# Last layers: the first six pieces of w_out issued ahead of the second unit's tokens, with the pieces' tiles laid out in reverse

## The chip, the cores and the metric

One core of one Trainium2 chip runs the whole program. The metric is the device time of one execution in microseconds; lower is better.

## The reference, cut to what matters

```python
def reference(**kwargs):
    attn_out = _attn_ref(**attn_kwargs)                    # pooled-key attention, 4 x 8 heads x 576 rows
    x = np.ascontiguousarray(attn_out.transpose(0, 2, 1, 3)).reshape(B * S, H * D)   # 2304 x 512
    x = _moe_ref(x=x, **moe_kwargs)                        # top-1 of 8 experts, with a capacity
    return _moe2_ref(x=x, **moe2_kwargs)

def _moe2_ref(x, w_in, w_out, s, b):                       # the last layers
    h = x @ w_in                                           # 512 -> 2048
    r = np.maximum(h, 0.0)
    g = s * (r * r) + b
    return (g @ w_out).astype(np.float32)                  # 2048 -> 512
```

## The kernel before, in words

The program has three stages: attention with the routing, the expert layers (`Experts.main`), and the last layers (`last_layers`). The last layers work on units of 256 tokens (`CU`). The weight `w_out` comes in as 64-bit floats, in 16 pieces of 128 rows (512 KB each): every piece is loaded as pairs of 32-bit words into a tile `wo[i]`, turned into a 32-bit float by four steps on VectorE and one on ScalarE (`Weights64.step`, L735 to L744), and split by ScalarE (L1258) and GpSimd (L1259) into a high and a low part, which lie in the same memory under the same name.

Order is written out by hand (`manual_schedule`): each engine runs its instructions in the order of the program, and a DMA asked for with `nc.sync` is issued by SP, in order as well.

The seam between the stages goes so. `last` (L1166) is the end of the expert stage; it runs inside nested conditionals on the number of small units. It loads the first unit's tokens (`load_y(0)`, two DMAs: L899 reads 512 KB from `yt` into `yr`, L900 reads the row numbers `it` from `idc`), computes the last small unit's second layer (L1114), stores its result (`store_small`: L991 to `yt`, L992 from the tile `ids_s` to `idc`), then asks for the second unit's tokens (`load_y(1)`), and runs the first four first-layer tiles of unit 0 (`EARLY`, L912). After the conditionals join, `last_layers` issues two small loads for the scalars s and b (`sb`, L1441), and `rest(0)` runs `unit(2)`, which calls `pair()`. That first asks for all 16 pieces of `w_out` (L1320), then runs `first(0, ...)`: for each of 16 tiles f it does the first layer (L912), `square` (L1273 on ScalarE, L1274 on VectorE), one or two conversion steps of `w_out` (`spare`), and `parts` (L1279 ScalarE, L1280 GpSimd). After it `split_y(1, ...)` splits the second unit's tokens (L904, L905), and `second(0, ...)` multiplies by the converted pieces (L1285). When all 16 pieces are converted, `spare` goes on to sum them (L1306, L1308); that sum, with b, makes the rows of dropped tokens (L1313, L1314).

Memory: the expert stage's tiles lie in two pools, `m1` and `m`, which are given back when that stage ends. The pool `n` of the last layers (`sb`, `y1h`, `y1l`, `c_f`, `c_u`, `gh`, `gl`, `wo`) takes their place, in the order in which its tiles are declared. By the sizes of the tiles, all `wo` lie in what was `m`: before, `wo0` to `wo4` over `hs`, `xg`, `idt` and `ids_s`, `wo5` to `wo8` over `vraw` (the experts' second weight), `wo9` to `wo12` over `kraw` (the first weight) and `wo13` to `wo15` over `c_raw`.

Of the kernel before, what the change touches and what calls it, by code (L numbers as in the profile page):

```python
# [10 lines left out]
I32 = mybir.dt.int32  # L11
# [9 lines left out]
DM = H * D  # L21
# [3 lines left out]
P = 128  # L25
# [10 lines left out]
KF2 = FF2 // P  # L36
# [712 lines left out]
class Experts:  # L749
# [176 lines left out]
    def main(self, left, one, ps):  # L926


        nc, tc, yt = self.nc, self.tc, self.yt
# [69 lines left out]
        def conv(n, end=cv.total):  # L999
            for _ in range(n):  # L1000
                if pos[0] < end:
                    if pos[0] == 3 or pos[0] % 4 == 2 and pos[0] > 6:
                        self.load_raw(max(3, pos[0] // 4 + 2), queue)
                    cv.step(pos[0])
                    pos[0] += 1

        def part(n):
            for _ in range(n):
                if parted[0] < KF:
                    self.split_in(parted[0])  # L1010
                    parted[0] += 1
# [100 lines left out]
        def small_layer2(f):  # L1112
            for d in range(KD):
                nc.tensor.matmul(py[d][:, :SM], lhsT=self.w2r[:, f, d * P:d * P + P], rhs=hs[f], start=f == 0, stop=f == KF - 1)  # L1114

        def store_small(s):
            store_y(sid(s), yo(s % 2, SM), self.ids_s[s % 4], SM, SSUB)
# [48 lines left out]
        def last(s):  # L1166

            early = cap >= SM + CU
            if early:
                self.load_y(0)  # L1170
            for f in range(KF):
                small_layer2(f)
                if early and f in (4, 5):
                    for k in range(2):
                        self.split_y(0, 2 * f - 8 + k, nc.vector)
                conv(2)
                part(1)
            store_small(s)
            if early:
                self.load_y(1)  # L1180
            conv(cv.total)
            if not early:
                self.load_y(0)
                for k in range(KD):
                    self.split_y(0, k, nc.vector)
                self.load_y(1)
            for f in range(EARLY):
                self.layer1_y(0, ps[f], self.w1h[:, f], self.w1l[:, f])

# [43 lines left out]
def last_layers(nc, tc, c, a, pool, x, ps, out):  # L1233
# [6 lines left out]
    sb = pool.tile([P, 2], F32, name="sb")  # L1240
# [3 lines left out]
    cf, cu = [pool.tile([P, DM], I32, name=f"c_f{i}") for i in range(2)], [pool.tile([P, DM], F32, name="c_u0")]  # L1244
    gh = pool.tile([P, KF2, CU], F32R, name="gh")
    gl = pool.tile([P, KF2, CU], F32R, name="gl")
    wo = [pool.tile([P, DM, 2], I32, name=f"wo{i}") for i in range(KF2)]
    ph, po = ps[0:4], ps[4:8]
    sums = {}
    slots = raw[2:4]  # L1250
# [13 lines left out]
    def conv(n):  # L1264
        for _ in range(n):
            if done[0] < cv.total:
                cv.step(done[0])
                done[0] += 1

    def square(f, p, n):  # L1270

        r = rt[f % 4][:, :n]
        nc.scalar.activation(r, p, AF.Relu)  # L1273
        nc.vector.scalar_tensor_tensor(out=r, in0=p, scalar=0.0, in1=r, op0=ALU.max, op1=ALU.mult)  # L1274

    def parts(f, n=CU, at=None):

        at = f if at is None else at
        nc.scalar.copy(gh[:, at, :n], rt[f % 4][:, :n])  # L1279
        nc.gpsimd.tensor_sub(gl[:, at, :n], rt[f % 4][:, :n], gh[:, at, :n])  # L1280

    def layer2(p, j, f, c=slice(0, DM), at=None):
        at = f if at is None else at
        for i, (l, z) in enumerate(((gh, 0), (gh, 1), (gl, 0))):
            nc.tensor.matmul(p[:, c], lhsT=l[:, at, j * P:j * P + P], rhs=wo[f][:, z, c], start=f == 0 and i == 0, stop=f == KF2 - 1 and i == 2)  # L1285
# [12 lines left out]
    def tokens(u):  # L1298
        if u < NV:
            for k in range(KD):  # L1300
                x.split_y(u, k, nc.gpsimd)

    def add(i):

        if i == 0:
            nc.vector.tensor_add(sums["acc"], wo[0][:, 0], wo[0][:, 1])  # L1306
        elif 1 < i < 2 * KF2:
            nc.vector.tensor_add(sums["acc"], sums["acc"], wo[i // 2][:, i % 2])  # L1308
# [8 lines left out]
    def pair():  # L1317

        for i in range(KF2):
            nc.sync.dma_start(out=wo[i].rearrange("p c two -> p (c two)"), in_=wout[:, i])  # L1320
        held = []
        adds = iter(range(2 * KF2))

        def spare(n):
            for _ in range(n):
                if done[0] < cv.total:
                    conv(1)
                    continue
                if "acc" not in sums:
                    nc.vector.memset(onesf, 1.0)  # L1330
                    sums["acc"] = pool.tile([P, DM], F32, name="c_f0")
                    slots.append(pool.tile([P, DM], F32, name="c_f1"))
                    sums["drop"] = pool.tile([P, DM], F32, name="c_u0")
                add(next(adds, 2 * KF2))

        def first(u, f0, f1, banks):
            for n, f in enumerate(range(f0, f1)):
                p = banks[f % len(banks)][:, :CU]
                if u or f >= EARLY:
                    x.layer1_y(u, p, *win[f])  # L1340
                square(f, p, CU)
                spare(2 if u == 0 and n % 4 == 3 else 1)
                if held:
                    parts(*held.pop())
                held.append((f, CU, f))
            parts(*held.pop())

        def second(u, f0, f1, n):
            for f in range(f0, f1):
                for j in range(2):  # L1350
                    layer2(po[2 * u + j], j, f, at=f)
                spare(n)

        first(0, 0, KF2, ps)
        for k in range(KD):
            x.split_y(1, k, nc.gpsimd)
        second(0, 0, KF, 2)
        first(1, 0, KF, ph)
        x.load_y(2)
        second(1, 0, KF, 2)  # L1360
        second(0, KF, KF2, 2)
        first(1, KF, KF2, ph)
        tokens(2)
        second(1, KF, KF2, 2)
        for i in adds:
            add(i)
# [56 lines left out]
    def rest(u):  # L1423
        if u == NV:
            return
        if u < 2:
            rest(2)
            return
        if u < SURE:
            unit(u)  # L1430
            rest(u + 1)
            return
        with tc.If(kept > u * CU + P) as cond:
            unit(u)
            rest(u + 1)
        with cond.Else():
            with tc.If(kept > u * CU):
                half(u)

    for i, n in enumerate(("moe2_s", "moe2_b")):  # L1440
        nc.sync.dma_start(out=sb[:, i:i + 1], in_=a[n].unsqueeze(0).to_broadcast([P, 1]))  # L1441
    rest(0)


# [44 lines left out]
```

## Time and profile before

| | us |
|---|---|
| median of 3 runs | 723.9 (717.18, 723.9, 726.66) |
| the profiled execution | 719.65 |
| its span, first to last instruction | 718.0 |

| engine | busy us | share of the span |
|---|---|---|
| PE (TensorE matmul) | 603.5 | 84% |
| PEld (weight load) | 559.9 | 78% |
| DVE (VectorE) | 391.8 | 55% |
| POOL (GpSimd) | 324.3 | 45% |
| ACT (ScalarE) | 254.3 | 35% |

Times in a trace count from the start of the span. PEld overlaps PE. A DMA's row in the timeline is the time SP needs to issue it, not the transfer. PEclk is the granted TensorE clock as a share of full speed. "Issue" is time in which an engine waited for nothing that the profile shows. Releasers are inferred from semaphores: where an instruction waits for several, the one that came last is named.

### The profile page before, as it was taken

To read this page: it belongs to the slowest core of one execution; us is meant where nothing else is said; L and a number is where in the kernel's file an instruction comes from. 1 tells how busy PE (TensorE), PEld (TensorE's weight loads), DVE (VectorE), ACT (ScalarE), POOL (GpSimd) and SP (SyncE) were. 2 spreads that over 40 slices of the span, in tenths; PEclk is the share of its full clock that TensorE was granted. 3 is DMA by queue.
4 is the path that set the end of the run, shared out by engine and by line. 5 is a ranking of instruction groups with operands and counts; after the bars stand their busy time and mean duration, and the time that the engine had idled before them with its cause. 6 is when DMAs were issued, how large, how long until landed. Compare 5 with 4: busy or idle time off the path is not lost. (4 is left out here: it accounts for less than half of the span.)

```text
span 718.0 us, 11212 instructions
## 1 busy us (share of the span) xinstructions
PE 603.5 (84%) x3943; PEld 559.9 (78%) x3943; DVE 391.8 (55%) x793; ACT 254.3 (35%) x617; POOL 324.3 (45%) x336
## 2 busy tenths in 40 slices
PE   6788787768599387996976768989999999999985
PEld 5677776768499387996976647877989989899885
DVE  4789699749688482444520877999332212021250
ACT  1354655335254344414320544432412304123030
POOL 5567455465363343502300784644473515335281
PEclk8899989689889698997799778999999999999998
DMA  8997997792539766583812920001730010100000
GB/s 168 197 180 134 154 183 235 103 272 63 94 92 181 240 154 214 56 290 107 279 34 53 405 89 0 1 1 30 264 104 15 14 46 1 45 16 2 32 1 18
DMA packets 78571, 81.97 MB, mean 114 GB/s; under 512 B 30732, under 2 KB 59404, under 8 KB 78476
## 3 DMA queue, kind: packets, MB, share of 16 engines
q1 hardware_dynamic: 67580, 67.19, 37.1%
q0 software_dynamic: 3184, 6.83, 4.0%
q10 hardware_dynamic: 7712, 6.84, 3.2%
q8 instruction: 41, 0.67, 0.5%
q14 instruction: 54, 0.44, 0.3%
HBM read 64.04 MB, written 17.62 MB: 114 GB/s over the span
## 5 line engine op out<-in xcount | busy, mean ns | idle before, releaser
L1285 PE MATMUL bank<-wo,gh 128*128 128x512 f32 (+1 forms) x448 | 135.0, 384 | 13.7 <-POOL wo L1259 9.0
L1280 POOL TENSOR_TENSOR gl<-rt,gh 128x256 fp32r<-128x256 f32 (+1 forms) x112 | 89.3, 806 | 95.5 <-ACT gh L1279 88.9
L1285 PEld LDWEIGHTS bank<-wo,gh 128*128 128x128 f32 x448 | 83.4, 193 | 32.4 <-POOL wo L1259 11.1
L1285 PE MATMUL bank<-wo,gl 128*128 128x512 f32 (+1 forms) x224 | 85.3, 381 | 0.0
L791 POOL TENSOR_TENSOR w1l<-kraw,w1h 128x512 fp32r<-128x512 f32 x40 | 54.3, 1375 | 59.9 <-ACT w1h L790 59.6
L986 PE MATMUL bank<-hs,w2h 128*128 128x288 f32 (+1 forms) x308 | 72.9, 327 | 7.3 <-issue 7.3
L986 PEld LDWEIGHTS bank<-hs,w2h 128*128 128x128 f32 x308 | 55.2, 209 | 8.1 <-issue 7.8
L1292 DVE SCALAR_TENSOR_TENSOR raw<-bank,sb,c_u 128x512 f32<-128x512 f32 (+1 forms) x14 | 9.9, 710 | 85.4 <-PE bank L1285 85.4
L1273 ACT ACTIVATE rt<-tq 128x256 f32<-128x256 f32 (+1 forms) x26 | 9.5, 367 | 114.6 <-PE tq L912 92.1
L1285 PEld LDWEIGHTS bank<-wo,gl 128*128 128x128 f32 x224 | 43.2, 193 | 7.6
L986 PE MATMUL bank<-hs,w2l 128*128 128x288 f32 (+1 forms) x148 | 47.1, 318 | 2.1 <-DVE w2l L795 2.1
L1279 ACT CAST gh<-rt 128x256 fp32r<-128x256 f32 (+1 forms) x112 | 43.0, 384 | 4.1 <-DVE rt L1274 4.1
L1274 DVE SCALAR_TENSOR_TENSOR rt<-bank,rt 128x256 f32<-128x256 f32 (+1 forms) x60 | 24.1, 403 | 36.3 <-ACT rt L1273 36.3
L1293 POOL DMA_INDIRECT out_dram<-raw,it x12 | 12.0, 1000 | 62.3 <-DVE raw L1292 61.8
L1273 ACT ACTIVATE rt<-bank 128x256 f32<-128x256 f32 (+1 forms) x60 | 22.2, 370 | 39.5 <-PE bank L912 26.8
L1259 POOL TENSOR_TENSOR wo<-c_f,wo 128x512 fp32r<-128x512 f32 x16 | 24.8, 1550 | 21.5 <-ACT wo L1258 21.5
L798 POOL DMA_INDIRECT xg<-xd,idt x15 | 18.1, 1205 | 34.9 <-DMA idt<-ids 32.1
L986 PEld LDWEIGHTS bank<-hs,w2l 128*128 128x128 f32 x148 | 30.7, 207 | 2.4 <-DVE w2l L795 2.4
L795 DVE TENSOR_TENSOR w2l<-vraw,w2h 128x512 fp32r<-128x512 f32 x39 | 32.1, 823 | 0.5 <-ACT w2h L794 0.2
L210 PE MATMUL sc<-kbd,qT 128*128 128x144 f32 (+1 forms) x152 | 26.0, 322 | 2.3 <-DVE r L267 2.3
L744 DVE SCALAR_TENSOR_TENSOR c_f<-c_u,c_f 128x512 f32<-128x512 f32 x24 | 25.3, 1055 | 4.8 <-ACT c_u L737 3.5
L1308 DVE TENSOR_TENSOR c_f<-c_f,wo 128x512 f32<-128x512 f32 x30 | 26.2, 875 | 0.8
(409 smaller groups left out, 1706.7 us busy)
## 6 DMA issues: line engine op xcount, KB each, us to landing
kraw<-in_moe_w_dram SPq DMA_DIRECT2D x24, 512.0 KB
vraw<-in_moe_w_dram SPq DMA_DIRECT2D x24, 512.0 KB
wo<-in_moe_w_out_dram SPq DMA_DIRECT2D x16, 512.0 KB
c_raw<-in_moe_w_in_dram ACTq DMA_DIRECT2D x13, 512.0 KB
kraw<-in_k_dram SPq DMA_DIRECT2D x8, 576.0 KB
out_dram<-c_u SPq DMA_DIRECT2D x1, 4608.0 KB
q<-in_q_dram SPq DMA_DIRECT2D x16, 256.0 KB
xd<-xr SPq DMA_DIRECT2D x16, 256.0 KB
```

The costliest lines, as they stand in the source:

```text
L210: nc.tensor.matmul(sc[:n, p // 2, p % 2 * 144:p % 2 * 144 + 144], lhsT=q[:, p, :n], rhs=kbd[b % 2][:, p], start=True, stop=True)
L744: v.scalar_tensor_tensor(out=f, in0=u, scalar=TINY, in1=f, op0=ALU.is_ge, op1=ALU.mult)
L791: eng.tensor_sub(self.w1l[:, i], self.w1(i), self.w1h[:, i])
L795: eng.tensor_sub(self.w2l[i], self.w2r[:, i], self.w2h[i])
L986: nc.tensor.matmul(py[d][:, :v.n], lhsT=l[f][:, d * P:d * P + P], rhs=r[f], start=f == 0 and i == 0, stop=f == KF - 1 and i == 2)
L1259: nc.gpsimd.tensor_sub(w[:, 1], f, w[:, 0])
L1273: nc.scalar.activation(r, p, AF.Relu)
L1274: nc.vector.scalar_tensor_tensor(out=r, in0=p, scalar=0.0, in1=r, op0=ALU.max, op1=ALU.mult)
L1279: nc.scalar.copy(gh[:, at, :n], rt[f % 4][:, :n])
L1280: nc.gpsimd.tensor_sub(gl[:, at, :n], rt[f % 4][:, :n], gh[:, at, :n])
L1285: nc.tensor.matmul(p[:, c], lhsT=l[:, at, j * P:j * P + P], rhs=wo[f][:, z, c], start=f == 0 and i == 0, stop=f == KF2 - 1 and i == 2)
L1308: nc.vector.tensor_add(sums["acc"], sums["acc"], wo[i // 2][:, i % 2])
```

## The change

`load_y(1)` is taken out of `last` and issued in `pair()`, behind the sixth of the 16 loads of `w_out`. The two loads of `sb` move from the end of `last_layers` to just behind it. Loads 6 to 15 follow. The tiles `wo` are declared from 15 down to 0, so `wo0` to `wo2` lie where `c_raw` was, `wo3` to `wo6` over `kraw`, `wo7` to `wo10` over `vraw`, and `wo11` to `wo15` over the rest. No arithmetic changes.

```diff
@@ in last()
             store_small(s)
-            if early:
-                self.load_y(1)
             conv(cv.total)
             if not early:
                 self.load_y(0)
                 for k in range(KD):
                     self.split_y(0, k, nc.vector)
-                self.load_y(1)
@@ in last_layers()
-    wo = [pool.tile([P, DM, 2], I32, name=f"wo{i}") for i in range(KF2)]
+    wo = [pool.tile([P, DM, 2], I32, name=f"wo{i}") for i in reversed(range(KF2))][::-1]
@@ in pair()
         for i in range(KF2):
             nc.sync.dma_start(out=wo[i].rearrange("p c two -> p (c two)"), in_=wout[:, i])
+            if i == 5:
+                x.load_y(1)
+                for j, n in enumerate(("moe2_s", "moe2_b")):
+                    nc.sync.dma_start(out=sb[:, j:j + 1], in_=a[n].unsqueeze(0).to_broadcast([P, 1]))
@@ at the end of last_layers()
-    for i, n in enumerate(("moe2_s", "moe2_b")):
-        nc.sync.dma_start(out=sb[:, i:i + 1], in_=a[n].unsqueeze(0).to_broadcast([P, 1]))
     rest(0)
```

## Rows read from the trace of the kernel before

**Rows 1.** Chain of waits, 376 to 405 us: start us, length us, what
```profile
377.85 8.82 DMA idc<-ids_s
386.69 3.35 DMA it<-idc
...
390.43 0.03 SPq L1441
...
390.56 0.35 SPq L1441
...
391.43 5.45 DMA wo<-in_moe_w_out_dram
...
397.29 0.43 DVE c_f L735
```

**Rows 2.** Waits by engine, 376 to 404 us: total us, times, longest us
```profile
DVE c_f L735 <- DMA wo<-in_moe_w_out_dram: 18.7, 1, 18.7
...
PE misc L912 <- DVE rt L1274: 9.1, 1, 9.1
```

**Rows 3.** Windows: stretch, length, busy us (instructions) of five engines, PEclk, DMA, GB/s
```profile
389.00:397.00 8.00, 0.02 (x1) 0.00 (x0) 0.00 (x0) 0.00 (x0) 0.00 (x0) 0.78 0.37 111
397.00:421.00 24.00, 19.65 (x107) 17.74 (x108) 22.59 (x36) 16.00 (x43) 21.99 (x19) 0.79 0.79 315
...
437.00:501.00 64.00, 60.45 (x366) 53.24 (x365) 56.96 (x78) 21.82 (x53) 32.80 (x29) 0.99 0.04 9
501.00:718.00 217.00, 205.22 (x1354) 188.44 (x1354) 50.80 (x106) 55.72 (x174) 92.29 (x118) 0.98 0.13 46
```

**Rows 4.** Timeline of SP, 340 to 480 us: start us, issue us, line, what, count
```profile
377.85 0.41 SPq L992 DMA_DIRECT2D idc<-ids_s  x1
382.67 0.39 SPq L899 DMA_DIRECT2D yr<-yt  x1
...
391.43 15.19 SPq L1320 DMA_DIRECT2D wo<-in_moe_w_out_dram  x16
426.53 0.38 SPq L899 DMA_DIRECT2D yr<-yt  x1
```

**Rows 5.** First uses of pool n's memory, by line: waiting instructions ahead of each
```profile
L1441 SPq EVENT_SEMAPHORE  x9: 27/28/28, 387.5 to 390.5; - x9
...
L735 DVEq EVENT_SEMAPHORE  x9: 49/50/50, 378.2 to 397.2; - x9
...
L1280 POOLq EVENT_SEMAPHORE  x8: 42/43/7539, 390.1 to 390.7; - x8
```

**Rows 6.** Timeline of SP, 355 to 366 us, an earlier store to idc
```profile
357.42 0.38 SPq L992 DMA_DIRECT2D idc<-ids_s  x1
365.34 0.38 SPq L1088 DMA_DIRECT2D ids_s<-ids  x1
```

**Rows 7.** DMA view, 426 to 434 us: GB/s in 40 slices of 0.2 us
```profile
GB/s 0 41 0 0 0 0 0 20 61 56 51 92 276 374 384 369 399 354 172 17 0 0 0 0 0 0 0 0 0 0 0 0 0 0 0 0 0 0 0 0
```

**Rows 8.** DMA view, 390 to 398 us: GB/s in 40 slices of 0.2 us
```profile
GB/s 0 0 0 0 0 0 0 0 0 1 0 0 0 0 0 0 0 0 0 21 164 123 41 62 103 82 266 451 389 410 471 410 348 471 451 389 410 451 430 348
```

**Rows 9.** Waits of SP's queue, 396 to 420 us: total us, times, longest us
```profile
SPq L1320 <- DMA wo<-in_moe_w_out_dram: 7.9, 8, 1.4
```

**Rows 10.** Timeline of ACT and of DVE: the tokens' split, piece 6's first conversion step
```profile
418.83 1.33 ACT L904 CAST y1h<-yr 128x256 fp32r<-128x256 f32 x4
...
427.75 1.49 DVE L735 TENSOR_SCALAR c_f<-wo 128x512 int32<-128x512 int32 x1 [2.52 <-POOL wo L1259]
```

**Rows 11.** DMA view, 376 to 392 us: GB/s in 40 slices of 0.4 us
```profile
GB/s 0 0 0 20 0 226 320 190 3 0 0 41 0 0 0 0 0 0 0 77 54 128 100 44 0 20 38 49 54 143 284 214 142 8 0 0 0 0 0 0
```

**Rows 12.** Chain of waits, whole span, where VectorE hands over to TensorE
```profile
500.33 0.69 DVE c_f L1308
501.02 0.35 DVE rt L1274
501.41 1.12 PE tq L1313 x2
...
522.68 21.77 PE bank L1285 x96
```

## The prediction

> **What bounds the kernel now.** I read the chain of waits first, then the waits by engine, then the windows, and only then single queues. The last 217 us are TensorE's: it is busy 205.22 of 217.00 us there [rows 3], and the chain there is made of its matmuls [rows 12]. Nothing in the change touches that part but its start. Before it, from 397 to 501 us, the chain lies mostly on VectorE, which converts and sums the 16 pieces of w_out: 22.59 busy of 24.00 us and then 56.96 of 64.00 us [rows 3], up to the sum's last step at 500.33 and the hand-over to TensorE at 501.41 [rows 12]. All that begins when the first piece of w_out is there: VectorE sat idle 18.7 us for it, and TensorE 9.1 us behind VectorE, because VectorE's next conversion step stands ahead of its `square` in program order and the banks fill up [rows 2]. In 389 to 397 us no engine does more than 0.02 us of work [rows 3]. So the stretch to look at is what leads to that first piece, and there the chain has four links [rows 1]: the store of row numbers to `idc`, issued at 377.85 and landed 8.82 us later, at 386.67; the load of `it` for the second unit, issued at 386.69, which must follow that store since it reads `idc`, and landed after 3.35 us, at 390.04; SP's remaining waits and the two `sb` issues, until 391.43; the first piece, 5.45 us, landed at 396.88. VectorE starts at 397.29.
>
> **What the change removes from that chain.** Both DMAs of `load_y(1)` and both of `sb` now stand behind six pieces. The `it` link, 3.35 us, goes. The two `sb` issues go: 391.43 less 390.56, 0.87 us [rows 1].
>
> **What stays ahead of the first piece.** It becomes the first use of the new pool's memory by SP, and takes over the waits that `sb` had. Those are a list of nine waiting instructions on SP; VectorE's first use of the pool has nine too, GpSimd's eight, although they touch different tiles [rows 5]. I read this as a list that belongs to the pool: whichever tile comes first waits for every user of the memory given back, whatever lies under its own bytes. The store to `idc` reads `ids_s`, which was in that memory, so its landing stays in the chain, and the reversed layout changes no wait. I cost the layout at nothing; what it would give if waits went tile by tile is the first rival.
>
> When does that store land? In this execution after 8.82 us [rows 1]; an earlier store of the same kind was issued at 357.42, and SP, which waited for it, could go on at 365.34 at the latest [rows 6], so 7.9 us or less. Here the load of `yr` was issued meanwhile, at 382.67 [rows 4], and moved at 44 to 128 GB/s from 383.6 to 385.6 [rows 11]; that may have held the store up, and it goes. Between the ends I take 8.5 us, 386.35; bounds 385.75 and 386.67. From there SP has between the last two waits (390.56 less 390.43, 0.13 us) and the whole list behind `it` (390.56 less 390.04, 0.52 us) to go [rows 1]. I take 0.2: the first piece is issued at 386.55 instead of 391.43.
>
> How long does it take? Before: 5.45 us [rows 1], but nothing moved until 393.8, 2.4 us after the issue, and then for 1.4 us only 21 to 164 GB/s; near full rate came at 395.2, 3.8 us after the issue [rows 8]. A 512 KB load with nothing ahead of it, the `yr` issued at 426.53 [rows 4], moved from 427.4, 0.9 us after the issue, was near full rate from 428.4, some 2.0 us after it, and ended by 430.0, 3.5 us after [rows 7]. The `sb` loads, two times 128 packets of 4 bytes, are what stood ahead before, and now stand behind. So 3.5 is the lower bound, 5.45 the upper; I take 4.3, nearer the lone load, and a little over it since five more pieces follow at once. The Trainium skill, page "DMA: Bandwidth & Descriptors", section "Anatomy of one DMA — SWDGE (gpsimd) path", gives some 2.0 us fixed plus the bytes at 436 GB/s, measured for DMAs that GpSimd issues; as an estimate 3.2 us for this load, which would make the gain below 7.1 us, and the lone load's row says that this is a little short.
>
> **The sum.** The first piece lands at 386.55 + 4.3 = 390.85 instead of 396.88: 6.0 us sooner. The bounds are 396.88 − (385.75 + 0.13 + 3.5) = 7.5 us and 396.88 − (386.67 + 0.52 + 5.45) = 4.2 us. The work behind it is the same, in the same order on each engine, and VectorE and GpSimd (21.99 of 24.00 us) are both full right behind it [rows 3], so all of it moves by that much. TensorE's stall shrinks from 9.1 to about 3 us, and its granted clock, 0.78 and 0.79 around the stall [rows 3], may fall less; I cost that at nothing, since VectorE sets the pace there.
>
> **What the moved DMAs cost.** Of SP's four moved issues none is waited for soon. The tokens `yr` are seventh in the queue: at the 410 GB/s of [rows 8] a 512 KB load takes 1.28 us, so they land at about 386.55 + 2.0 + 7 × 1.28 = 397.5. Their first reader, L904, ran at 418.83 [rows 10] and would now run at 412.8: 15 us of cover. `sb` is first read behind the sum, past 501 us [rows 12]. Before, eight of the sixteen w_out issues waited for an earlier one, 1.4 us at most [rows 9], so I read eight DMAs in flight as SP's limit. Now `sb` is ninth and tenth, and SP, with pieces 6 to 15 queued behind, waits for pieces 0 and 1. Piece 6 can then be issued when piece 2 has landed, some 2.6 us behind piece 0, at 393.5, and lands by about 402 even behind all that is in flight. Its first conversion step, at 427.75 before [rows 10], would come at 421.7: 20 us of cover. Without cover, each would cost its lateness one for one, as ScalarE and VectorE run in order.
>
> So 719.65 − 6.0 = 713.7 us for an execution like the profiled one (span 718.0, and 1.65 around it). That one lies 4.25 under the median of the runs shown; against the median the forecast is 723.9 − 6.0 = 717.9 us.
>
> **Rivals.**
> *The pieces go at once.* If a tile waits only for what lay under its own bytes, the first piece need not wait for the store. SP began the list for `sb` at 387.5, 0.8 us after it issued `it` at 386.69 [rows 1, 5]; 0.8 us after 377.85 is 378.65. With 5.45 us, since the expert stage's last store is then still moving (up to 320 GB/s from 378 to 379.2 [rows 11]), it lands at 384.1: 12.8 us gained, 711.1 against the median, 1.8% less. For it speaks the intention of the layout, against it the three long lists [rows 5].
>
> *Nothing gained.* If the six pieces' packets share the engines, the first is complete only with the last: 386.55 + 2.0 + 6 × 1.28 = 396.2, 0.7 us gained, 723.2. Against it: before, the first landed 1.7 us after full rate began though others were queued behind it [rows 1, 8].
>
> *The tokens come too late, and the kernel is slower.* `yr` is behind 3 MB. If the seven transfers ran not at 410 but at some 110 GB/s, as `yr` itself did in its poor stretch [rows 11], it would take 7 × 4.77 = 33.4 us: landing at 422.0, 9.2 us after 412.8, so 719.65 − 6.0 + 9.2 = 722.9, or 727.1 against the median. It is slower than before from a landing at 418.8 on, and by 2% only from about 433. Against it: the loads of w_out ran at 410 GB/s from their start [rows 8]. By the Trainium skill, same page, section "Queues, rings and completion order", an engine takes descriptors in ring order, so that tokens behind six pieces do wait for them all; the first piece's late start behind the small loads [rows 8] agrees.
>
> **How the numbers follow.** The forecast 0.76, pieces at once 0.08, nothing gained 0.10, tokens late 0.06. Two per cent, 14.5 us, is about what a measurement of this kernel can tell from no change; the three runs shown span 9.5 us. The forecast's own range is 723.9 − 7.5 = 716.4 to 723.9 − 4.2 = 719.7, before the runs' scatter. With it: the lowest run less the most, 717.18 − 7.5 = 709.7, which takes in the pieces at once; the highest less the least, 726.66 − 4.2 = 722.5. Nothing gained at 723.2 and the late tokens are left out, 0.16. Faster by over 2%: half of the pieces at once and a little scatter, 0.06. Slower by over 2%: 0.03. Within: 0.91.
>
> **What would show it.** In the changed kernel's chain the store to `idc` should be followed directly by the first w_out load, with no `it` and no `sb` between; that load issued near 386.5 and landed in 3.5 to 5.45 us; VectorE's idle before L735 down from 18.7 to about 12.7 us; the hand-over at 501.41 near 495.4; L904 not waiting for its load. I am wrong if the first load is issued near 379 (waits go by tile), if it takes 9 us or more (shared engines), if L904 or L735 waits for a DMA again, or if 501.41 moves less than the first landing does.

## The result, and the profile after

The changed kernel takes 714.74 us (median of 20 runs, 704.76 to 721.37) where the kernel before takes 722.57 us in the same comparison (20 runs, 717.03 to 726.92): 7.8 us less. The ratio is 0.9843, interval 0.9802 to 0.9884. Timed again later (the run `a1_after_again` below) it was 714.36 against 721.23 us, 6.9 us less, ratio 0.9934, interval 0.9898 to 0.9971. The ratios leave disturbed runs out, not as many on both sides, which is why they lie further apart than the medians; one profile below, that of `sb` alone (e2), is of such a run. The two intervals do not overlap (8.4 to 14.3 us by the first, 2.1 to 7.4 us by the second), so the size of the gain rests on the rows of the seam more than on the totals. The forecast was a gain of 6.0 us. The profiled execution took 706.86 us, span 705.1.

The chain of waits of the changed kernel, at the seam and at the hand-over (start us, length us, what); it answers [rows 1] and [rows 12]:

```profile
373.21 7.28 DMA idc<-ids_s
...
380.63 4.35 DMA wo<-in_moe_w_out_dram
...
385.01 0.05 DVEq L735
...
385.69 0.05 DVEq L735
...
385.79 0.43 DVE c_f L735
...
489.94 1.13 PE tq L1310 x2
```

The store of row numbers is followed directly by the first piece of `w_out`; the load of `it` and the two `sb` issues are gone from between. The store landed after 7.28 us, SP needed 0.14 us (380.63 less 373.21 + 7.28), the piece 4.35 us. From the issue of the store, the first piece lands 380.63 + 4.35 − 373.21 = 11.77 us later, where [rows 1] give 391.43 + 5.45 − 377.85 = 19.03: 7.3 us sooner. VectorE then passes eight waiting instructions from 385.01 on and starts 0.81 us behind the landing; before it was 397.29 − 396.88 = 0.41. The hand-over to TensorE comes 489.94 − 373.21 = 116.73 us behind the store's issue, before 501.41 − 377.85 = 123.56: 6.8 us sooner.

The timeline of SP in the changed kernel (start us, issue us, line, what, count), which answers [rows 4]:

```profile
372.51 0.40 SPq L991 DMA_DIRECT2D yt<-yo  x1
373.21 0.39 SPq L992 DMA_DIRECT2D idc<-ids_s  x1
380.63 3.06 SPq L1317 DMA_DIRECT2D wo<-in_moe_w_out_dram  x6
383.74 0.45 SPq L899 DMA_DIRECT2D yr<-yt  x1
...
389.18 9.51 SPq L1317 DMA_DIRECT2D wo<-in_moe_w_out_dram  x10
```

Lines 1188 to 1320 of before are numbered three lower in the changed kernel: L1317 is L1320 of before, L1271 is L1274, L1277 is L1280 and L1310 is L1313. Between 373.6 and 380.6 SP issues nothing. The waits of SP's queue say why (first row below: total us, times, longest us), and the waits by engine what became of the two of [rows 2]:

```profile
SPq L1317 <- DMA idc<-ids_s: 4.1, 1, 4.1
```

```profile
DVE c_f L735 <- PE tq L912: 11.3, 1, 11.3
...
ACT c_u L737 <- DMA wo<-in_moe_w_out_dram: 10.1, 1, 10.1
...
PE misc L912 <- DVE rt L1271: 1.6, 1, 1.6
```

VectorE's idle time ahead of L735 fell from 18.7 to 11.3 us (it is put down to TensorE, although the piece of `w_out` landed last; ScalarE's first conversion step names that piece), TensorE's behind VectorE from 9.1 to 1.6. The instructions by line show that SP's and GpSimd's lists of [rows 5] stand as they were, only before other tiles:

```profile
L1317 SPq EVENT_SEMAPHORE  x9: 28/28/28, 374.6 to 380.6; - x9
...
L1277 POOLq EVENT_SEMAPHORE  x8: 43/43/6028, 373.8 to 380.6; - x8
```

The windows (length, busy us of PE, PEld, DVE, ACT, POOL, PEclk, DMA share, GB/s), which answer [rows 3]:

```profile
386.00:410.00 24.00, 17.69 (x104) 15.61 (x105) 22.89 (x36) 16.12 (x44) 22.57 (x19) 0.86 0.83 326
...
426.00:489.00 63.00, 60.19 (x365) 53.33 (x365) 55.81 (x77) 21.57 (x53) 32.39 (x29) 1.00 0.03 9
489.00:705.00 216.00, 203.47 (x1354) 186.63 (x1354) 51.67 (x106) 55.96 (x175) 92.20 (x118) 0.99 0.13 46
```

The stretches behind the seam hold the same work in the same time: from VectorE's first L735 to the hand-over it is 489.94 − 385.79 = 104.15 us, before 501.41 − 397.29 = 104.12. The granted clock of the first 24 us is 0.86 where it was 0.79, and that stretch is no shorter for it.

**Where the 12.9 us between the two profiled spans (718.0 and 705.1) are.** Up to the issue of the last store of `idc` 377.85 − 373.21 = 4.64; from there to the hand-over 6.83; from the hand-over to the end 1.4. Only the second part can be the change. Most of the first is there already at the first store of outputs of the expert stage, at 179.6 where it was 183.6. Over the eleven profiled executions whose program is the same up to there (all but the three with the order of the stores swapped) that store came at 174.4 to 185.1. And from the hand-over to the end all fourteen executions lie at 215.1 to 215.3 or at 216.3 to 216.8 us, the changed kernel's own two profiles at 215.1 and 216.5. These two are scatter, and a comparison of two spans would have credited the change with them.

### The profile page after: what moved, and what is told of

It is laid out like the page before. It is cut to its first block, busy times and chain, and to the rows that moved or that the text cites. A ratio compares the mean times of both kernels' runs of the same rounds, so it can differ in the third digit from the quotient of the medians.

```text
span 705.1 us, 11212 instructions
## 1 busy us (share of the span) xinstructions
PE 594.7 (84%) x3943; PEld 551.3 (78%) x3943; DVE 382.1 (54%) x793; ACT 254.3 (36%) x617; POOL 324.2 (46%) x336
## 3 DMA queue, kind: packets, MB, share of 16 engines
q0 software_dynamic: 3184, 6.83, 4.5%
## 5 line engine op out<-in xcount | busy, mean ns | idle before, releaser
L1277 POOL TENSOR_TENSOR gl<-rt,gh 128x256 fp32r<-128x256 f32 (+1 forms) x112 | 89.4, 807 | 88.0 <-ACT gh L1276 80.7
L1271 DVE SCALAR_TENSOR_TENSOR rt<-bank,rt 128x256 f32<-128x256 f32 (+1 forms) x60 | 24.1, 402 | 36.1 <-ACT rt L1270 36.1
L1256 POOL TENSOR_TENSOR wo<-c_f,wo 128x512 fp32r<-128x512 f32 x16 | 24.8, 1550 | 21.5 <-ACT wo L1255 21.5
L210 PEld LDWEIGHTS sc<-kbd,qT 128*128 128x128 f32 (+1 forms) x152 | 22.6, 206 | 10.5 <-issue 9.6
L255 PE MATMUL o<-vx,eT 128*128 128x146 f32 (+1 forms) x144 | 24.4, 317 | 6.6 <-DVE u_sum L569 3.1
```

What stands on the lines that cost most here:

```text
L210: nc.tensor.matmul(sc[:n, p // 2, p % 2 * 144:p % 2 * 144 + 144], lhsT=q[:, p, :n], rhs=kbd[b % 2][:, p], start=True, stop=True)
L1256: nc.gpsimd.tensor_sub(w[:, 1], f, w[:, 0])
```

## The experiments

All kernels in one table, worked out from each profiled execution; landings are the last semaphore event of a transfer in the trace. All times are us, "after" is after the issue of the last store of outputs (`yt`), which every variant has. The last column is the stretch from the first to the last of these stores, which lies ahead of the seam.

| kernel | store of indices took | first piece issued, after | it took | VectorE's L735 starts, after | end, after | expert stage's stores |
|---|---|---|---|---|---|---|
| before | 8.83 | 14.27 | 5.45 | 20.13 | 340.8 | 193.6 |
| the change | 7.28 | 8.12 | 4.35 | 13.27 | 332.5 | 192.9 |
| a1 (the change again) | 7.45 | 8.29 | 4.81 | 13.90 | 334.6 | 193.6 |
| e1 tokens moved only | 6.90 | 8.62 | 8.17 | 17.40 | 336.6 | 195.5 |
| e2 `sb` moved only | 8.17 | 12.89 | 3.67 | 17.16 | 338.5 | 198.2 |
| e3 plain layout | 7.32 | 8.15 | 5.14 | 14.10 | 335.5 | 193.5 |
| e8 tokens and `sb` behind all 16 | 6.80 | 7.63 | 5.94 | 14.39 | 335.4 | 195.5 |
| e4 waits by tile | 8.63 | 2.15 | 9.80 | 11.97 | 332.5 | 193.5 |
| e5 waits by tile, plain layout | 7.58 | 2.21 | 9.19 | 11.42 | 330.8 | 191.9 |
| e9 waits by tile, ScalarE's queue | 8.33 | 1.51 | 9.94 | 20.94 | 340.2 | 196.0 |
| e10 waits by tile, no indices stored | none | 1.11 | 4.32 | 5.55 | 326.8 | 186.8 |
| e6 indices stored first | 5.91 | 4.53 | 3.76 | 9.10 | 328.5 | 184.8 |
| e7 indices first, waits by tile | 6.00 | 1.44 | 6.24 | 7.71 | 328.3 | 187.0 |
| a2 (e7 again) | 7.91 | 1.44 | 7.65 | 9.12 | 328.4 | 186.1 |

From L735's start to the end it is 319.2 to 321.4 us in all fourteen: whatever the seam gains arrives at the end, give or take 1.1 us. Each row is one execution. Where one kernel was profiled twice, L735's start differs by 0.6 us (the change and a1) and by 1.4 us (e7 and a2); smaller differences between rows show nothing.

**Which part brings it: the tokens alone.** The second unit's tokens go behind the sixth piece, `sb` stays ahead, and the tiles lie in plain order.

```diff
 # the changed kernel, with
             if i == 5:
                 x.load_y(1)
-                for j, n in enumerate(("moe2_s", "moe2_b")):
-                    nc.sync.dma_start(out=sb[:, j:j + 1], in_=a[n].unsqueeze(0).to_broadcast([P, 1]))
...
+    for i, n in enumerate(("moe2_s", "moe2_b")):
+        nc.sync.dma_start(out=sb[:, i:i + 1], in_=a[n].unsqueeze(0).to_broadcast([P, 1]))
     # ahead of rest(0), as before; wo in plain order
```

> Of the change, only the second unit's tokens move behind the sixth piece; the two sb loads stay ahead of the first piece, the layout stays as before. Counted from the issue of the store to idc in the seam; before the first piece landed 19.0 us after it, in the changed kernel 11.8. My theory (the it link is gone, sb still costs its two issues and its place in the queue): store 7.3 to 8.8, waits 0.1, sb issues 0.9, first piece 5.4: landing 13.7 to 15.2 us after the store's issue, so 4 to 5 of the 7.3 us. Rival (the tokens are all of it, sb was free): 11.8 us. Time: 3 to 6 us under the kernel before.

Measured: 717.27 us against 720.85, ratio 0.9918 (0.9867 to 0.9969). The piece landed 16.1 us after the store of indices was issued, later than the 13.7 to 15.2 expected: the two `sb` issues cost SP 0.9 us, and the piece behind them took 8.17. SP's timeline in this kernel, and its DMA view from 388 to 400 us in slices of 0.3 us:

```profile
388.30 0.36 SPq L1440 DMA_DIRECT2D sb<-in_moe_s_dram  x1
388.71 0.42 SPq L1440 DMA_DIRECT2D sb<-in_moe_b_dram  x1
389.18 4.36 SPq L1317 DMA_DIRECT2D wo<-in_moe_w_out_dram  x6
```

```profile
GB/s 0 0 0 0 0 0 0 0 0 0 0 0 0 0 0 0 28 123 164 192 464 382 369 410 410 410 423 410 410 423 410 437 423 437 410 396 423 423 423 410
```

For 3.6 us behind the issue of the first piece nothing moves, then for 1.2 us little, and full rate comes at 394.0. That is the pattern of [rows 8], in which the prediction saw the two small loads at work.

**The other part: `sb` alone.** The `sb` loads go behind the sixth piece, and the tokens' loads stay in `last`.

```diff
 # the changed kernel, with, in last()
             store_small(s)
+            if early:
+                self.load_y(1)
...
 # and in pair(), where sb stays; wo in plain order
             if i == 5:
-                x.load_y(1)
```

> Of the change, only the two sb loads move behind the sixth piece; the tokens' loads stay ahead of the first piece, the layout stays as before. My theory: store 8.8 (slowed by the load of yr beside it), it 3.3, waits 0.2 to 0.5, first piece 4.3 (nothing small ahead of it in the queue): landing 16.5 to 17.0 us after the store's issue, so 2 to 2.5 us of the 7.3. Rival A (sb ahead of it is not why the first piece took 5.45 us): 18.0 us. Rival B (the store's 8.8 us was scatter, not the load beside it): the store lands after 7.3 to 7.8 us here too, landing 15.5 us. Time: about 2 us under the kernel before.

Measured: 718.53 us against 720.85, ratio 0.9896 (0.9841 to 0.9951). Its chain of waits:

```profile
380.47 8.17 DMA idc<-ids_s
388.65 3.50 DMA it<-idc
...
392.67 3.67 DMA wo<-in_moe_w_out_dram
```

The `it` link is there again, with the `yr` load beside the store; but with nothing small ahead of it the piece took 3.67 us. It landed 15.9 us behind the store's issue, not the 16.5 to 17.0 expected, because I had it at 4.3 us. Rival B has the landing about right (15.5) and the reason wrong: the store took 8.17 us, not 7.3 to 7.8. So each part alone moves L735 by 2.7 and 3.0 us, both together by 6.9 (6.2 in a1, 6.0 in e3 below): in e1 the gain of the missing `it` goes partly into the piece behind `sb`, in e2 the gain of the piece stays behind `it`. This split rests on the profiles; the intervals of the three ratios (e1, e2, e3) overlap.

**The layout.** Only the tiles' order is put back.

```diff
-    wo = [pool.tile([P, DM, 2], I32, name=f"wo{i}") for i in reversed(range(KF2))][::-1]
+    wo = [pool.tile([P, DM, 2], I32, name=f"wo{i}") for i in range(KF2)]
```

> The changed kernel without the reversed layout. My theory (the list of waits belongs to the pool, the layout changes none): SP's first piece again follows the landing of the store to idc, 11.8 us from the store's issue to the first piece's landing, time as the changed kernel. Rival (the layout gives part of the gain): the first piece lands 1 us or more later than in the changed kernel.

Measured: 710.9 us against 720.85, ratio 0.9852 (0.9808 to 0.9897). SP's timeline:

```profile
373.71 0.39 SPq L992 DMA_DIRECT2D idc<-ids_s  x1
381.17 4.27 SPq L1317 DMA_DIRECT2D wo<-in_moe_w_out_dram  x6
```

The first piece is issued 7.46 us behind the store, in the changed kernel 7.42, and lands 12.6 us behind it (11.8 and 12.4 in the two profiles of the change), so the rival's 1 us is not there. The layout removes no wait.

**Waits by tile.** The pool `n` is told to let each tile wait only for the users of the memory under its own bytes. This is the first rival made true.

```diff
-            pool = es.enter_context(tc.tile_pool(name="n", bufs=1))
+            pool = es.enter_context(tc.tile_pool(name="n", bufs=1, reuse_waits="tile"))
```

> The changed kernel, but the pool of the last layers is declared so that each of its tiles waits only for the users of what lay under its own bytes. My theory (the pool's list alone holds the first piece, its bytes have been free since the weights of the small units were converted): the list of nine is gone, the first piece is issued 0.8 to 1.5 us after the store to idc and lands 5.2 to 7.0 us after it instead of 11.8; VectorE starts as much sooner, all behind it follows, 5 to 6.5 us under the changed kernel. Rival (something else is ready no sooner, such as the split of the first tokens or TensorE's first tiles): VectorE's first conversion step moves by less than 3 us.

Measured: 710.86 us against 720.85, ratio 0.9876 (0.9829 to 0.9923). SP's timeline, and the DMA view from 367 to 383 us in slices of 0.4 us (first row: busy share of the DMA engines in tenths):

```profile
367.91 0.40 SPq L991 DMA_DIRECT2D yt<-yo  x1
368.60 0.39 SPq L992 DMA_DIRECT2D idc<-ids_s  x1
370.06 5.68 SPq L1317 DMA_DIRECT2D wo<-in_moe_w_out_dram  x6
```

```profile
DMA  0000399210999500996999365231797999999999
GB/s 0 20 0 0 99 328 298 13 20 0 164 72 61 31 0 0 195 72 31 31 41 51 10 41 51 20 31 31 236 277 307 451 369 410 379 440 420 410 440 410
```

The list of waits is gone: the first piece is issued 1.46 us behind the store, 6.0 us sooner. But it took 9.80 us instead of 4.35. From 373.8 to 378.2, with four to six pieces asked for, only 10 to 72 GB/s moved, although the DMA engines were busy for 0.6 of the time or more until 375.8 (0.1 to 0.6 after it). Rates above 200 began at 378.2, 1 us behind the landing of the store of indices at 377.23. The piece landed 2.6 us behind that store. The expected landing (5.2 to 7.0 us behind the store's issue; measured 11.25) fell, and with it the 5 to 6.5 us that this kernel was to be under the changed one: L735 starts 1.3 to 1.9 us sooner, and the median is that of e3. Most of the wait had moved from SP's list into the DMA engines. Two theories were left: the 144 writes of 4 bytes each hold the engines, whatever is asked for behind them; or they hold only what stands behind them in SP's queue.

**The same through another queue.** The first six pieces are issued by ScalarE, on its own queue.

```diff
-            nc.sync.dma_start(out=wo[i].rearrange("p c two -> p (c two)"), in_=wout[:, i])
+            (nc.scalar if i < 6 else nc.sync).dma_start(out=wo[i].rearrange("p c two -> p (c two)"), in_=wout[:, i])
...
-            pool = es.enter_context(tc.tile_pool(name="n", bufs=1))
+            pool = es.enter_context(tc.tile_pool(name="n", bufs=1, reuse_waits="tile"))
```

> Tile by tile waits, and the first six pieces asked for through ScalarE's queue; the store to idc and all else stay on SP's. Theory A1 (order within one queue holds the pieces behind the small store): the first piece passes it, lands 3.7 to 5.5 us after its issue and 5.5 to 7.5 us after the store's issue instead of 11.3, VectorE starts 4 to 6 us sooner, the time is 4 to 6 us under tile by tile waits alone. Theory A2 (the DMA engines themselves are held by the small writes, whatever the queue): the first piece lands after the store to idc again, 10 us or more after that store's issue, no gain.

Measured: 722.05 us against 722.75, ratio 1.007 (1.0027 to 1.0114). The timeline of SP, that of ScalarE, and the instructions of L1317 on ScalarE (duration in ns, least, median and most):

```profile
380.12 0.49 SPq L992 DMA_DIRECT2D idc<-ids_s  x1
```

```profile
380.94 18.59 ACTq L1317 DMA_DIRECT2D wo<-in_moe_w_out_dram  x6
399.58 0.39 ACT L1270 ACTIVATE rt<-tq 128x256 f32<-128x256 f32 x1 [20.18 <-DMA wo<-in_moe_w_out_dram]
```

```profile
L1317 ACTq DMA_DIRECT2D wo<-in_moe_w_out_dram x6: 334/358/574, 380.9 to 399.2; - x6
```

The piece took 9.94 us and landed 2.4 us behind the store of indices again, although it stood in another queue. So it is not the order in SP's queue that holds the piece, but something that both queues share. That agrees with the Trainium skill, page "DMA: Bandwidth & Descriptors", section "Issuing engines are not separate DMA queues": DMAs of all issuing engines run on the same 16 DMA engines. It also says that issuing on several engines saves only the usually small time of the issue; here it cost. The six issues took 0.33 to 0.57 us each, but between them ScalarE waited for earlier transfers to land: by the trace the third went 0.15 us behind the landing of the store of outputs (386.88), the fourth and fifth 0.06 and 0.02 us behind the first and second piece (390.88 and 392.15), and the sixth, at 399.17, 0.02 us behind a load of `sb`. So ScalarE was in them from 380.94 to 399.53, idle for 20.2 us ahead of its first `square`, and VectorE's L735 behind that came 9.5 us after its piece (20.94 − 11.45): more than the earlier issue gave.

The Trainium skill, same page, section "Queues, rings and completion order", states that a transfer's semaphore comes only after every earlier write of that DMA engine, across queues. The landings behind the store, here and above, agree. It is not the whole of it: by the GB/s row of the waits by tile the bytes moved late as well, not only their semaphores.

**No indices at all.** Waits by tile, and the small units' indices aren't stored.

```diff
-            nc.sync.dma_start(out=self.idc[cols(u, ids.shape[1] * sub)]...)
+            if sub == SUB:
+                nc.sync.dma_start(out=self.idc[cols(u, ids.shape[1] * sub)]...)
...
-            pool = es.enter_context(tc.tile_pool(name="n", bufs=1))
+            pool = es.enter_context(tc.tile_pool(name="n", bufs=1, reuse_waits="tile"))
```

> Waits by tile as in the run that took away the list of nine, and the small units' indices (144 writes of 4 bytes each) aren't stored at all, so that the rows of the small units' tokens are missing from the output. Theory (the small writes hold the DMA engines): the first piece, issued some 1.5 to 2.5 us after the store of outputs, takes 5 to 6.5 us in place of 9.8, and lands 7 to 8.5 us after the issue of that store, where it was 11.95. Rival (six pieces asked for within 6 us hold each other up, or the store of outputs does): it still takes 9 us or more.

Measured, one run: 697.85 us. SP's timeline, and the DMA view from 367 to 383 us in slices of 0.4 us:

```profile
369.26 0.40 SPq L991 DMA_DIRECT2D yt<-yo  x1
370.37 3.18 SPq L1318 DMA_DIRECT2D wo<-in_moe_w_out_dram  x6
```

```profile
GB/s 20 0 0 0 0 0 0 0 297 323 128 61 102 236 276 317 348 379 195 154 369 369 440 420 440 399 399 420 379 430 399 420 440 374 371 364 348 217 107 44
```

The piece took 4.32 us, less than the 5 to 6.5 expected, and landed 5.43 us behind the issue of the store of outputs (7 to 8.5 expected); rates above 200 began at 372.2, 1.8 us behind the issue, with the store of outputs still under way. The rival (six pieces hold each other up) falls. By these two profiles a store of 576 bytes in 144 writes costs the first piece 9.80 − 4.32 = 5.5 us.

**The layout, once waits go by tile.**

```diff
-    wo = [pool.tile([P, DM, 2], I32, name=f"wo{i}") for i in reversed(range(KF2))][::-1]
+    wo = [pool.tile([P, DM, 2], I32, name=f"wo{i}") for i in range(KF2)]
...
-            pool = es.enter_context(tc.tile_pool(name="n", bufs=1))
+            pool = es.enter_context(tc.tile_pool(name="n", bufs=1, reuse_waits="tile"))
```

> Waits by tile, and the pieces laid out in their plain order, so that the first six take the memory of c_raw, kraw and part of vraw, whose last readers in the run with waits by tile are done about 336, 356 and 367 us, all ahead of the store of outputs. Theory: with waits by tile the layout costs no wait either: the first piece is issued 1.4 to 2 us after the store of indices and lands 10.5 to 12 us after it, as with the reversed layout (1.46 and 11.25). Rival (the reversed layout is what lets the first pieces go): the first piece is issued 3 us or more after that store.

The expectation named the wrong memory: in plain order it is `wo0` to `wo4` that lie over `hs`, `xg`, `idt` and `ids_s`. Measured, one run: 708.7 us; the first piece was issued 1.51 us behind the store of indices and landed 10.70 us behind it, as with the reversed layout (1.46 and 11.25). The waits of SP's queue show what the layout is worth then:

```profile
SPq L1317 <- DMA idc<-ids_s: 4.0, 1, 4.0
```

Four pieces go at once, the fifth, over `ids_s`, waits 4.0 us for the store. With the reversed layout all six go within 5.68 us. Since VectorE needs the first piece first, the end does not show it (330.8 and 332.5 us behind the store of outputs).

**The indices first.** If these writes are the first piece's last obstacle, they should go as early as they can. `ids` are known before the small unit's result, and only the order of two lines kept their store behind the store of outputs.

```diff
         def store_y(u, y, ids, n, sub):
             for d in range(KD):
                 nc.scalar.copy(y[:, d], py[d][:, :n])
+            nc.sync.dma_start(out=self.idc[...], in_=ids)
             nc.sync.dma_start(out=self.yt...[:, :, cols(u, n)], in_=y)
-            nc.sync.dma_start(out=self.idc[...], in_=ids)
```

> The changed kernel, but each result of the expert stage has its row numbers stored to idc ahead of its 288 or 576 KB store to yt instead of behind it. Counted from the issue of that yt store in the seam; in the changed kernel the store to idc went out 0.7 us and the first piece 8.1 us after it, and the piece landed 12.5 us after it. My theory (what the first piece now waits for is the landing of the store to idc): it can go out as soon as the it load of the first unit has landed, some 3 us ahead of the yt store, and lands 4 to 5 us after it; then the yt store's own landing (3.8 to 5.5 us) ends the list: first piece issued 4.5 to 5.5 us after the yt store, landed 9 to 10 us after it, 2.5 to 3.5 us sooner than in the changed kernel. Rival (the two stores together fill the queue, their order does not matter): first piece issued 7 us or more after the yt store.

Measured: 700.66 us against 722.75, ratio 0.9803 (0.9683 to 0.9923). SP's timeline:

```profile
364.79 0.39 SPq L991 DMA_DIRECT2D idc<-ids_s  x1
369.66 0.40 SPq L992 DMA_DIRECT2D yt<-yo  x1
374.19 4.59 SPq L1317 DMA_DIRECT2D wo<-in_moe_w_out_dram  x6
```

The list now waits for the store of outputs (4.39 us), and the piece lands 8.3 us behind that store's issue (9 to 10 expected) instead of 12.5. That is 4.2 us; the median, of four runs, says 14 us less than the changed kernel's. Most of the rest lies ahead of the seam, which had not been expected: from the first to the last store of outputs of the expert stage it is 184.8 us here, and 191.9 to 198.2 in the ten other runs that store all their indices behind the outputs. A row of SP's waits from 180 to 368 us of the kernel before shows one place:

```profile
SPq L1130 <- DMA idc<-idt: 8.8, 1, 8.8
```

That wait of 8.8 us, which the changed kernel has too (8.7), is no longer among the longest of SP's waits in this run. How much of the 8 us it makes up was not tried.

**Both.** The indices first, and waits by tile.

> Tile by tile waits and the row numbers stored ahead of yt. With tile by tile waits alone the first piece was issued 1.5 us after the store to idc but took 9.8 us to land, 2.6 us behind that store. Theory A (the pieces stand behind the store to idc in SP's queue, whose 144 writes of 4 bytes take their 7 to 9 us whoever waits): with that store some 3 us earlier, the first piece lands 2.5 us behind it again, 7 to 8.5 us after the issue of the yt store, against 12.0 with tile by tile waits alone. Theory B (the transfers ahead, not the small store, hold the piece): 11 us or more.

Measured: 699.77 us against 722.75, ratio 0.9715 (0.9584 to 0.9846); the piece landed 7.7 us behind the issue of the store of outputs, within theory A's 7 to 8.5. Its mechanism holds only in part: the piece came 5.25 us behind the landing of the store of indices (371.03), not 2.5. The store of outputs took 6.39 us here, 3.72 us in the kernel without indices; whether it holds the piece too was not separated. And beside e6 (700.66) the times show nothing of the waits by tile, although L735 starts 1.4 us sooner. Again, beside the changed kernel on one chip:

> The changed kernel once more, beside the kernel of the next entry on the same chip. Seam theory: it is faster than before by 6 to 8.5 us (ratio 0.985 to 0.992); in its profile the first piece is issued 7.3 to 8.5 us after the issue of the last small unit's store of indices, and lands 11.5 to 13 us after it, where before it was 19.0. Rival (the gain of the first profile was scatter of the first 370 us): the landing would be seen at 15 us or later, and the ratio above 0.995.

> The kernel with both further edits (the store of indices ahead of that of the outputs, and waits by tile) once more, on the chip that times the changed kernel. If the store of indices is what the first piece comes after, the first piece lands 7 to 8.5 us after the issue of the store of outputs, against 12.5 in the changed kernel, and the kernel is faster than the changed one by 3 to 6 us: ratio to before 0.978 to 0.986. Rival (the piece is held by the store of outputs as much as by the indices): it lands at 10 us or later, and the ratio is that of the changed kernel.

Measured: the changed kernel 714.36, this one 703.34, before 721.23 us; ratios to before 0.9934 (0.9898 to 0.9971) and 0.9782 (0.9729 to 0.9835). The changed kernel's first piece was issued 7.60 us behind the store of indices and landed 12.4 us behind it, as expected, 6.6 us sooner than before; its ratio lies a little over the expected 0.985 to 0.992 and under the rival's 0.995. In the other kernel SP's timeline reads:

```profile
371.85 0.39 SPq L991 DMA_DIRECT2D idc<-ids_s  x1
374.15 0.40 SPq L992 DMA_DIRECT2D yt<-yo  x1
375.59 6.65 SPq L1317 DMA_DIRECT2D wo<-in_moe_w_out_dram  x6
```

Here the indices were stored only 2.30 us ahead of the outputs (3.56 in the earlier run, 369.66 − 364.79 = 4.87 in the run before), and the store of outputs took 8.12 us, the piece 7.65; it landed 9.1 us behind the issue of the store of outputs, between the 7 to 8.5 expected and the rival's 10, and 3.5 us behind the landing of the store of indices. So the rival, that the store of outputs holds the piece as well, is not ruled out here, though e10 speaks against it. This version beats both kernels, by 2.2% (just within the expected ratio) and, against the changed one, by 11.0 us, where 3 to 6 were expected: in the two profiles L735 starts 4.8 us sooner (13.90 − 9.12), and the expert stage's stores, which the expectation left out, take 193.6 − 186.1 = 7.5 us less.

**The cover of the tokens.** Tokens and `sb` go behind all sixteen pieces.

```diff
-            if i == 5:
+            if i == KF2 - 1:
```

> The changed kernel with the second unit's tokens and sb behind all 16 pieces instead of behind six. This prices the rival of late tokens. In the changed kernel the 16 pieces landed until 408.6 and the tokens' first reader L904 ran at 407.3. Theory (one queue, in order, 1.28 us for 512 KB): the tokens land 36 to 37 us after the store to idc, L904 needs them 34.1 us after it; it waits 2 to 3 us, and ScalarE's conversion steps behind it with it, so the hand-over to TensorE comes 1 to 3 us later than in the changed kernel. Rival (tokens move past the pieces in the queue): L904 does not wait, no loss.

Measured: 716.74 us against 722.75, ratio 0.9943 (0.9879 to 1.0008). The timelines of SP and of ScalarE:

```profile
378.87 15.21 SPq L1317 DMA_DIRECT2D wo<-in_moe_w_out_dram  x16
395.04 0.38 SPq L899 DMA_DIRECT2D yr<-yt  x1
```

```profile
407.17 1.32 ACT L904 CAST y1h<-yr 128x256 fp32r<-128x256 f32 x4
```

The tokens landed at 405.46, 33.5 us behind the store of indices where 36 to 37 were expected, and so 1.7 us ahead of L904, which ran 21.5 us behind L735, as in every kernel here. They had not moved past the pieces: the last of these landed at 404.04 by the trace. Even behind 8 MB the tokens cost nothing; what this kernel lost against the change (1.1 us at L735, no more than two profiles of one kernel differ by) is its first piece's 5.94 us.

## Why the prediction was right, step by step

*The links that go.* Right. `it` and `sb` left the chain, and nothing took their place. The two parts alone moved L735 by 2.7 and 3.0 us, the whole by 6.0 to 6.9.

*The store's landing: 8.5 us, bounds 7.9 to 8.82.* Mis-sized, and the bound was wrong. It took 7.28 and 7.45 us in the two profiles of the change, 6.80 to 7.32 in the three other runs that have no load beside it. The step that failed is the lower bound: [rows 6] said that the earlier store had landed after 7.9 us *or less*, a bound from above, and I used it as one from below. That the `yr` load holds the store up agrees with the runs: with it, 8.17 in e2 and 8.83 before, which no run without a load beside the store reaches.

*SP's 0.2 us.* 0.14 and 0.15.

*The piece's 4.3 us, bounds 3.5 to 5.45.* 4.35 and 4.81. Over the kernels that issue it behind the list and without `sb` ahead it is 3.67 to 5.94, so the upper bound was a little low. The kernels that issue it within 0.2 us of the landing of the store of indices have 4.35 to 5.94; the two whose store had landed 3.5 and 4.0 us earlier (e6 and e2) have 3.76 and 3.67. That the store slows the piece a little even after its landing is what this suggests; it was not tested. The estimate of 3.2 us worked out from the Trainium skill, page "DMA: Bandwidth & Descriptors", section "Anatomy of one DMA — SWDGE (gpsimd) path", is below all of them. That the two `sb` loads cause a late start as in [rows 8] is borne out by the two pairs that differ in the place of `sb` alone: 8.17 in e1 against 5.14 in e3, and 5.45 before against 3.67 in e2, one profile each.

*The sum: 6.0 us, 4.2 to 7.5.* The first landing came 7.3 us sooner in the first profile (1.2 of the 1.3 missing is the store's 8.5 against 7.28) and 6.6 in the second. A term was left out: VectorE's own list behind the landing, 0.4 us more than before. So the hand-over gained 6.8 and 6.1 us, and the medians 7.8, just over the range, and 6.9. The forecast of the time itself, 717.9 us with a range of 716.4 to 719.7, is 3.2 us over the measured 714.74, which only the range widened by the runs' scatter (709.7 to 722.5) holds: 1.8 us of it are the larger gain, 1.3 the three runs shown, whose median (723.9) lies over that of twenty (722.57).

*The layout at nothing, the list belonging to the pool.* Right; e3 shows it, and e4 that the list was the reason. The first rival was priced at 12.8 us, though, as if the list were all that holds the piece. With the list gone, L735 gained 8.2 us on before. That price was wrong in its mechanism: it let the piece run beside the store of indices at the 5.45 us of [rows 1].

*The cover of the tokens: landing 397.5, L904 at 412.8.* They landed at 394.43, L904 ran at 407.33: 12.9 us of cover against 15. With the 4.64 us by which this execution was ahead at the seam both agree within 2 us. That SP holds eight DMAs in flight held as well: the seventh piece went at 389.18, 0.01 us behind the landing of the third in the trace. The rival of the late tokens fell.

*TensorE's stall down to about 3 us.* 1.6 us. The granted clock stayed higher, 0.86 against 0.79, and gave nothing between L735 and the hand-over (104.15 us against 104.12), where VectorE sets the pace.

*"Nothing gained"* fell: the first of six pieces did not come with the last. *The end moves with the first landing*: it moves with L735's start in all fourteen executions, within 1.1 us, and L735 follows the landing by 0.02 to 0.8 us in all but e9, where `square` on VectorE stood ahead of it and waited for ScalarE.

## What to carry to other kernels

When a stage starts late, follow the chain back through the DMA queue and look there for small transfers: what one link of a few hundred bytes costs is paid by everything that is asked for behind it. Taking away a wait helps only as far as the resource behind it is free, so ask what the freed transfer will run beside: here most of the wait went from a list of semaphores into the DMA engines, and the larger gain came from storing the small thing earlier. A row that says "landed by" bounds a time from above only.

## What the runs showed of the hardware

A store of 144 values of 4 bytes each takes 5.9 to 8.8 us, and delays 512 KB loads issued 0.8 to 1.5 us behind it, from either queue: 9.8 us (e4), 9.2 (e5) and 9.9 (e9) where the load takes 4.3 without the store (e10). The movement of the small packets is not what takes the time. In the changed kernel, whose store was issued at 373.21 and landed at 380.49, the DMA view has the packets of under 512 bytes between 374.3 and 374.6 us (first row), and none from 374.6 to 380.5 us (second row):

```profile
DMA packets 222, 0.03 MB, mean 98 GB/s; under 512 B 172, under 2 KB 222, under 8 KB 222
...
DMA packets 2, 0.02 MB, mean 4 GB/s; under 512 B 0, under 2 KB 0, under 8 KB 0
```

What goes on between the last small packet and the landing, and why it slows other loads, stays open. Two loads of 128 times 4 bytes ahead of a 512 KB load make it 8.17 us instead of 5.14 in one pair of kernels (e1, e3) and 5.45 instead of 3.67 in another (before, e2). Six issues of 0.33 to 0.57 us each kept ScalarE for 18.59 us (e9), because it waited between them for earlier transfers to land; SP was through the same six in 5.68 us (e4).
